# Pooled attention and a gated convolution FFN on one core: six late gates by Sigmoid, two attention tiles with eight exponentials, additions in other pieces, a new order

## The chip, the cores and the metric

One core of one Trainium2 chip. The metric is the device time of one execution in microseconds (us), as the median of several runs. The engines are called as the profile calls them: PE (matrix products; PEld is its loading of weights), DVE (vector), ACT (scalar functions), POOL (general, here mostly the issuer of loads) and SP (issuer of DMAs).

## The reference

Keys and values are averaged over 8 neighbours (576 positions to 72), attention runs over the 72, and its output x goes through a feed-forward block with a gate that is a convolution over three neighbouring positions.

```python
k_p = k.reshape(B, H, Sp, pool, D).mean(axis=3)          # B, H, S, D = 8, 8, 576, 64; pool = 8
v_p = v.reshape(B, H, Sp, pool, D).mean(axis=3)
scores = scale * np.matmul(q, k_p.transpose(0, 1, 3, 2))
scores = scores - np.max(scores, axis=-1, keepdims=True)
attn = np.exp(scores)
attn = attn / (np.sum(attn, axis=-1, keepdims=True) + 1e-09)
x = np.matmul(attn, v_p)                                  # then heads side by side: 576 x 512
h = np.maximum(x @ w_in, 0.0)                             # 512 -> 1024
conv_out[:, s] = sum over k of conv_w[k] * h[:, s + k - 1]
gate = 1.0 / (1.0 + np.exp(-conv_out))
out = (h * gate) @ w_out                                  # 1024 -> 512
```

## The kernel before

**Work and tiles.** The eight batches form four groups g of two. The 1152 rows of a group make nine attention tiles t of 128 rows (group 0 has ten, its middle one cut in two). A tile goes through `att_scores` (PE), `att_max` (DVE, largest score of each of the 8 heads, negated), `att_shift` (subtracts it, by DVE into `sd`, or by PE for the ten tiles of group 0), `att_exp` (ACT), the turn of e (`att_turn` on PE with `att_copy`, or `att_send` by a transposing DMA on SP, groups 2 and 3), `att_values` (PE), `att_divide` (DVE) and the turn of x (`att_turn_out` and `att_copy_out`, or `att_out` on SP) into `xT`.

**The FFN of a batch b.** Its 1024 channels are eight blocks fb of 128, in two halves f4 of four. `ffn_in` (PE) multiplies by w_in, in two halves of 288 columns, `ffn_relu` (ACT) writes `hT`. The convolution has two forms. `ffn_conv` (PE) multiplies by diagonal matrices `dw`; a pair of blocks is written crosswise, so half of the result has its 64-row halves exchanged. `ffn_tap`, for (b, f4) = (4,1), (5,0), (5,1), (6,0), (6,1), (7,0), scales the middle tap on ACT and adds the two others on DVE, in `tg`; before them `ffn_wrap` copies 63 columns at both ends (POOL). Then ACT takes tanh of half the sum (`ffn_tanh`, `ffn_tap_tanh`), DVE adds 1 (`ffn_gate`, which also exchanges the halves back, L892 and L894, or L842) and multiplies by `hT` (L902, L843), into `gT`; `hT` holds half of h, since sigmoid(z) = (1 + tanh(z/2))/2. `ffn_out` (PE, 128 rows by 512 columns, eight products) needs all gates of its batches; ACT or DVE copies the result and SP or ACT issues the stores, two of 128 KB for each tile.

**What sets the order.** Every step is an `Op` of a graph, with its steps before it and its buffers. `Graph.ORDER` is a written list of numbers: 2 x step + engine choice (-1 takes a filling product from the spares), `FORMS` gives the form of some PE steps and `PLACES` the buffer of each ring. The steps are issued in that order; each engine then runs its own in order, held by semaphores. PSUM has eight banks, from which scores, turns, products and convolutions all draw.

**Start.** POOL issues the loads of q, k and v, of w_in and w_out; DVE clears buffers; PE pools the keys of batches 0 and 1 by a matrix `pm` (`prep_k`), keys of the others are added up by DVE (`pool_pair`, L406) and turned on PE.

```python
    def order(self):
        for n in self.ORDER:
            o = spares.pop(0) if n < 0 else self.ops[n // 2]
            o.engine = list(o.engines)[0 if n < 0 else n % 2]
...
    def ffn_tap_gate(b, f4):
        nc.vector.tensor_scalar(out=gate, in0=gate, scalar1=1.0, scalar2=None, op0=OP.add)
        nc.vector.tensor_tensor(out=gate, in0=gate, in1=h_of(b)[:, four], op=OP.mult)
```

## Time and profile before

| what | us |
| --- | --- |
| median of 3 runs (lowest, highest) | 218.12 (217.75, 218.72) |
| the profiled execution | 219.54 |
| its span | 217.8 |
| busy: PE, DVE, ACT, POOL | 198.8, 192.0, 161.8, 45.2 |
| granted clock of PE, mean | 0.998 |

A row of a group reads: line, engine, operation, output <- inputs, shapes, count | busy us, mean ns of one | idle time of the engine just before it, and what ended most of it. A row of the windows reads: stretch, length, then busy us and count of PE, PEld, DVE, ACT and POOL, the granted clock, the DMA share and GB/s. A row of the chain: start, length, what. Issuing of DMAs is not counted as busy; in the timeline it stands as SPq or ACTq. Matmul ends are modelled, so busy PE is not PE at its peak.

### The profile page before, as it was taken

What the parts mean: (1) busy time and instruction counts of PE and PEld (TensorE: products, weight loads), DVE (VectorE), ACT (ScalarE), POOL (GpSimd) and SP (SyncE); (2) the same over time, 40 slices, a digit from 0 to 9 for tenths busy, and PEclk for the clock granted to TensorE, in tenths of its full rate; (3) what the DMA queues carried; (4) which work ended last, traced back from release to release, by engine and by line L of the source; (5) the groups of instructions that cost most, each with busy time, mean ns of one, the idle gap of its engine ahead of it and who ended that gap; (6) DMA issues with size and microseconds to landing.
All of it is one profiled execution on the core that took longest, in us unless ns stands there. A gap on an engine that the chain in (4) does not pass through costs nothing.

```text
span 217.8 us, 6553 instructions
## 1 busy us (share of the span) xinstructions
PE 198.8 (91%) x2704; PEld 137.7 (63%) x2723; DVE 192.0 (88%) x334; ACT 161.8 (74%) x274; POOL 45.2 (21%) x81
## 2 busy tenths in 40 slices
PE   0597999998999999999999999999999999999990
PEld 0465778776587788667686775666566657545550
DVE  6859988999999899999999999899999999999310
ACT  2136677599989889678759877799889989987330
POOL 7951331033203120000000003103115113520000
PEclk9999999999999999999999999999999999999999
DMA  5999999999999998968865544674573555074864
GB/s 68 172 195 207 208 206 209 205 208 206 209 207 196 203 198 125 133 146 128 175 141 109 83 102 87 117 159 89 125 156 71 122 123 127 0 167 94 222 170 123
DMA packets 48834, 32.62 MB, mean 150 GB/s; under 512 B 28300, under 2 KB 44324, under 8 KB 48804
## 3 DMA queue, kind: packets, MB, share of 16 engines
q0 software_dynamic: 16288, 16.26, 45.8%
q1 hardware_dynamic: 31556, 14.50, 33.1%
q10 hardware_dynamic: 960, 1.44, 2.7%
q8 instruction: 21, 0.34, 0.6%
q14 instruction: 9, 0.07, 0.1%
HBM read 32.52 MB, written 9.44 MB: 193 GB/s over the span
## 4 chain that ended last, share of the span: by engine, by line
PE 50%; DVE 28%; ACT 9%; issue 7%; DMA 4%; POOL 1%; DVEq 0%; ACTq 0%; POOLq 0%
PE psum L910 21%; PE psum L694 17%; DVE negm L575 5%; DVE x L664 5%; DVE sd L587 4%; DMA kk<-in_k_dram 4%; ACT qT L501 3%; PE psum L649 3%; DVE gT L894 2%; PE psum L856 2%; DVE gT L902 2%; DVE v L453 2%; DVE r L662 2%; PE psum L624 2%; DVE kk L406 1%
## 5 line engine op out<-in xcount | busy, mean ns | idle before, releaser
L694 PE MATMUL psum<-xT,w_in_sb 128*128 128x288 bf16 x512 | 71.1, 286 | 0.1
L910 PE MATMUL psum<-w_out_sb,gT 128*128 128x512 bf16 (+1 forms) x277 | 65.0, 373 | 1.3 <-issue 0.5
L694 PEld LDWEIGHTS <-w_in_sb 128*128 128x128 bf16 x512 | 47.9, 98 | 14.2 <-issue 0.2
L703 ACT ACTIVATE hT<-psum 128x576 bf16<-128x576 f32 x64 | 40.7, 649 | 11.6 <-PE psum L694 11.1
L910 PEld LDWEIGHTS <-gT 128*128 128x128 bf16 x296 | 27.7, 98 | 27.7 <-issue 0.7
L831 DVE SCALAR_TENSOR_TENSOR tg<-hT,convw,tg 128x576 f32<-128x576 bf16 x48 | 37.7, 816 | 0.8
L575 DVE TENSOR_REDUCE negm<-psum 128x8 f32<-128x576 f32 (+2 forms) x37 | 27.5, 750 | 3.0 <-PE psum L562 1.7
L778 POOL COPY hT<-hT 128x126 bf16<-128x126 bf16 x16 | 9.4, 589 | 94.2 <-ACT hT L703 78.6
L664 DVE TENSOR_TENSOR x<-psum,r 128x512 bf16<-128x512 f32 (+1 forms) x37 | 25.6, 691 | 1.3
L587 DVE TENSOR_TENSOR sd<-psum,negm 128x576 f32<-128x576 f32 x27 | 20.1, 752 | 1.1 <-ACT gT L836 0.5
L856 PE MATMUL psum<-hT,dw 64*64 64x288 bf16 (+2 forms) x608 | 20.0, 261 | 0.5 <-DVE sd L587 0.3
L649 PE MATMUL psum<-vm,eT 128*128 128x65 bf16 (+5 forms) x240 | 19.0, 222 | 0.7 <-DVE vm L457 0.3
L613 ACT ACTIVATE e<-sd 128x576 bf16<-128x576 f32 x27 | 18.3, 689 | 1.1 <-DVE sd L587 1.1
L856 PEld LDWEIGHTS <-dw 64*64 64x64 bf16 x608 | 15.3, 107 | 5.8 <-issue 4.6
L829 ACT ACTIVATE tg<-hT,convw 128x576 f32<-128x576 bf16 x24 | 18.3, 774 | 0.1
L649 PEld LDWEIGHTS <-eT 128*128 128x128 bf16 (+1 forms) x240 | 15.0, 100 | 4.3 <-issue 1.8
L836 ACT ACTIVATE gT<-tg 128x576 bf16<-128x576 f32 x24 | 16.1, 681 | 1.6 <-DVE tg L831 0.9
L921 ACT COPY osb<-psum 128x512 f32<-128x512 f32 x25 | 14.6, 585 | 2.7 <-PE psum L910 2.3
L881 ACT ACTIVATE gT<-psum 128x576 bf16<-128x576 f32 x20 | 12.9, 647 | 3.8 <-PE psum L856 3.8
L881 ACT ACTIVATE tg<-psum 128x576 bf16<-128x576 f32 x20 | 13.0, 648 | 2.5 <-PE psum L856 1.8
L902 DVE TENSOR_TENSOR gT<-gT,hT 128x2304 bf16<-128x2304 bf16 x10 | 13.4, 1352 | 0.1
L453 DVE TENSOR_TENSOR v<-v 128x1280 bf16<-128x1280 bf16 (+2 forms) x24 | 12.9, 539 | 0.2
(83 smaller groups left out, 231.2 us busy)
## 6 DMA issues: line engine op xcount, KB each, us to landing
out_dram<-osb SPq DMA_DIRECT2D x54, 128.0 KB, 2.4
v<-in_v_dram POOLq DMA_DIRECT2D x8, 512.0 KB, 15.6
qp<-in_q_dram POOLq DMA_DIRECT2D x7, 576.0 KB, 13.9
kk<-in_k_dram POOLq DMA_DIRECT2D x3, 1152.0 KB, 13.5
out_dram<-qp ACTq DMA_DIRECT2D x10, 128.0 KB, 2.4
w_in_sb<-in_moe_w_in_dram POOLq DMA_DIRECT2D x2, 512.0 KB, 16.6
w_out_sb<-in_moe_w_out_dram POOLq DMA_DIRECT2D x1, 1024.0 KB, 22.1
out_dram<-qp SPq DMA_DIRECT2D x6, 128.0 KB, 2.4
```

Source lines behind the costliest of these rows:

```text
L575: nc.vector.tensor_reduce(out=a["m"][0:rows], in_=a["s"][0:rows, :, 0:2 * KW].rearrange("p a (h s) -> p a h s", s=Sp), axis=AX.X, op=OP.ma ...
L587: nc.vector.tensor_tensor(out=a["d"][0:rows], in0=a["s"][0:rows, :, 0:2 * KW].rearrange("p a (h s) -> p a h s", s=Sp), in1=a["m"][0:rows]. ...
L613: nc.scalar.activation(out=dst, in_=src, func=ACT.Exp, scale=1.0 / (POOL * 8.0),)
L649: nc.tensor.matmul(out=a["o"][lo:hi, h // 4, (h % 4) * (D + 1):(h % 4 + x1 - x0) * (D + 1)], lhsT=a["eT"][:, j, lo:hi], rhs=buf("vm", b)[: ...
L664: nc.vector.tensor_tensor(out=a["x"][0:rows].rearrange("p (a h d) -> p a h d", a=2, d=D), in0=ov[:, :, :, 0:D], in1=r[0:rows].unsqueeze(3) ...
L694: nc.tensor.matmul(out=banks(ps)[:, j, 0:SC], lhsT=w_in_block(dc, fb), rhs=buf("xT", g)[:, dc, i * S + j * SC:i * S + (j + 1) * SC], start ...
L703: nc.scalar.activation(out=h_of(b)[:, fb].rearrange("p (a s) -> p a s", a=2), in_=banks(ps)[:, :, 0:SC], func=ACT.Relu, scale=0.5,)
L829: nc.scalar.activation(out=acc, in_=h, func=ACT.Identity, scale=w)
L831: nc.vector.scalar_tensor_tensor(out=acc, in0=h, scalar=w, in1=acc, op0=OP.mult, op1=OP.add)
L856: nc.tensor.matmul(out=banks(pss[r ^ c])[c * D:(c + 1) * D, j, lo:hi], lhsT=dw[r * D:(r + 1) * D, tap * n_fb + fb, :], rhs=hT[r * D:(r + 1 ...
L881: nc.scalar.activation(out=t.rearrange("p (a s) -> p a s", a=2), in_=banks(ps)[:, :, 0:SC], func=ACT.Tanh, scale=0.5,)
L910: nc.tensor.matmul(out=bank(ps)[0:rows, columns], lhsT=buf("gT", g)[:, fb, t * P:t * P + rows], rhs=w_out_sb[:, fb, columns], start=(fb == 0),
```

## The change

1. **Six gates by Sigmoid.** The gates of both halves of batches 5, 6 and 7 are made by `ACT.Sigmoid`; `hT` then holds h itself (scale 1.0 in the ReLU), and the addition of 1 falls away. For (7,1), by `ffn_conv`, the exchange of halves stays, as a plain copy. The Sigmoid needs another function table than Exp and Tanh, so ACT loads a table a second time, and all exponentials come ahead of the first Sigmoid.
2. **Two tiles with eight exponentials.** For (g, t) = (3,1) and (3,8) the maximum is not subtracted ahead; ACT takes eight exponentials of 72 columns out of PSUM, each with the head's negated maximum as its bias. Tiles (0,5) and (0,9) go from subtraction by PE to DVE. The scale 1/64 moves from the exponential into the pooled keys.
3. **Additions in other pieces.** The three parts of `ffn_gate` are steps of their own, each on DVE or ACT (there `Identity` with a column of ones as bias). ACT has four of those before batch 4 and one of (7,1).
4. **Other engines and forms.** Six ReLUs run on DVE; five of twelve wraps on ACT; (4,0) and (7,1) are convolved without wraps, with 32 products for a pair of blocks in place of 24; tiles (1,0) and (1,3) turn x by DMA, (2,3) turns e on PE; five stores of the middle part go from SP to ACT; there are 11 filling products in place of 3, all within the start.
5. **ORDER, FORMS and PLACES are written anew**, so steps of all kinds stand at other places.

Counted over the whole program, on DVE: additions `gT<-gT` of 128x2304 from 6 to 1, of 128x1152 from 10 to 8, `gT<-tg` of 64x1152 from 20 to 15 and one copy of that shape. ACT issues 12 DMAs of stores before and 21 after, POOL makes 32 copies for wraps before and 14 after, and SP issues nine DMAs of stores fewer.

The start, on ACT, from its first instruction to the first exponential. Before:

```order
L1018 ACT_TABLE_LOAD
L1018 CAST gT_120<-ident 128x128
L398 CAST kT_80<-psum 64x2x72 x4
L501 COPY qT_77<-psum 128x2x320
L613 ACTIVATE e_96<-psum 128x576
```

With the change:

```order
L1025 ACT_TABLE_LOAD
L1025 CAST gT_120<-ident 128x128
L523 COPY qT_78<-psum 128x2x256
L418 CAST kT_81<-psum 64x2x72 x2
L523 COPY qT_78<-psum 128x2x320
L647 ACTIVATE e_97<-psum 128x576
```

Two of the four casts of the pooled keys (kT) of batch 0 have moved to DVE, and ACT has one more copy of its queries.

The middle part, on ACT, in the FFN of batches 1 and 3 beside the attention of groups 1 and 2. Before:

```order
L613 ACTIVATE e_99<-sd_126 128x576
L881 ACTIVATE gT_119<-psum 128x576
L881 ACTIVATE tg_116<-psum 128x576
L703 ACTIVATE hT_115<-psum 128x576
L613 ACTIVATE e_101<-sd_128 128x576
L703 ACTIVATE hT_115<-psum 128x576 x2
L881 ACTIVATE tg_117<-psum 128x576
L881 ACTIVATE gT_120<-psum 128x576
L921 COPY osb_124<-psum 128x512
```

With the change:

```order
L744 ACTIVATE hT_116<-psum 128x576
L647 ACTIVATE e_97<-sd_127 128x576
L817 ACTIVATE gT_121<-tg_117,ones 64x2x576
L744 ACTIVATE hT_116<-psum 128x576 x2
L946 DMA out_dram<-osb_122 64x512 x2
L883 ACTIVATE gT_120<-psum 128x576
L647 ACTIVATE e_99<-sd_128 128x576
L883 ACTIVATE tg_117<-psum 128x576
L934 COPY osb_125<-psum 128x512
```

An addition with ones and the two DMAs of a store now stand between ReLUs, tanhs and exponentials.

The end, on DVE, from the last multiplication of batch 6 to that of batch 7 (hT_114 is batch 7's before, hT_115 with the change). Before:

```order
L842 TENSOR_SCALAR gT_120<-gT_120 128x4x576
L843 TENSOR_TENSOR gT_120<-gT_120,hT_115 128x4x576
L831 SCALAR_TENSOR_TENSOR tg_117<-hT_114,convw,tg_117 128x576
L831 SCALAR_TENSOR_TENSOR tg_116<-hT_114,convw,tg_116 128x576 x2
L892 TENSOR_SCALAR gT_120<-gT_120 128x2x576
L894 TENSOR_SCALAR gT_120<-tg_118 64x2x576 x2
L842 TENSOR_SCALAR gT_120<-gT_120 128x4x576
L843 TENSOR_TENSOR gT_120<-gT_120,hT_114 128x4x576
L902 TENSOR_TENSOR gT_120<-gT_120,hT_114 128x4x576
```

With the change:

```order
L915 TENSOR_TENSOR gT_120<-gT_120,hT_116 128x4x576 x2
L845 SCALAR_TENSOR_TENSOR tg_117<-hT_115,convw,tg_117 128x576 x2
L845 SCALAR_TENSOR_TENSOR tg_119<-hT_115,convw,tg_119 128x576 x2
L934 COPY qp_73<-psum 128x512
L845 SCALAR_TENSOR_TENSOR tg_117<-hT_115,convw,tg_117 128x576
L845 SCALAR_TENSOR_TENSOR tg_118<-hT_115,convw,tg_118 128x576
L845 SCALAR_TENSOR_TENSOR tg_117<-hT_115,convw,tg_117 128x576
L845 SCALAR_TENSOR_TENSOR tg_118<-hT_115,convw,tg_118 128x576
L934 COPY osb_123<-psum 128x512
L819 COPY gT_120<-tg_119 64x2x576
L915 TENSOR_TENSOR gT_120<-gT_120,hT_115 128x4x576 x2
```

The additions ahead of the multiplications are gone but for one copy of half rows; both multiplications of batch 6 stand ahead of all taps of batch 7, and all its eight taps and two copies of outputs behind them.

The diff, cut to its core (the tables of numbers left out):

```diff
+        "shift": {
+            (0, 0): 1, (0, 1): 1, (0, 2): 1, (0, 3): 1, (0, 4): 1, (0, 6): 1, (0, 7): 1, (0, 8): 1, (3, 1): 2, (3, 8): 2,
+        },
...
+        "sigma": {
+            (5, 0): 1, (5, 1): 1, (6, 0): 1, (6, 1): 1, (7, 0): 1, (7, 1): 1,
+        },
...
     ORDER = (
-        6, 28, 14, 2, 24, 4, 26, 10, 34, 16, 36, 20, 22, 12, 104, 108, 106, 8, 38, 32, 18, 30, 40, 92, 56, 42, 58, -1, 44, 97,
...
+        6, 18, 14, 24, 2, 28, 4, 10, 16, 36, 20, 34, 8, 40, -1, 12, -1, 108, 26, 22, 111, -1, 42, 32, -1, -1, -1, 30, 46, -1,
...
-        nc.vector.memset(pm[0:TB, :, 0:Sp], 1.0)
+        nc.vector.memset(pm()[0:TB, :, 0:Sp], SCALE)
...
     def att_exp(g, t):
         a, rows = att[g, t], rows_of(g, t)
         e = a["e"] = buf("e", g, t)
+        if graph.chosen("shift", g, t) == 2:
+            for x in range(2):
+                for h in range(4):
+                    at = h // 2 * 2 * KW + x * KW + h % 2 * Sp if a["by_rows"] else (4 * x + h) * Sp
+                    nc.scalar.activation(
+                        out=e[0:rows, at:at + Sp],
+                        in_=a["s"][0:rows, x, h * Sp:(h + 1) * Sp],
+                        func=ACT.Exp,
+                        bias=a["m"][0:rows, x, h:h + 1],
+                        scale=1.0,
+                    )
+            return
...
-            scale=1.0 / (POOL * 8.0),
+            scale=1.0,
...
+    def ffn_relu(b, fb, ps, o):
+        out = h_of(b)[:, fb].rearrange("p (a s) -> p a s", a=2)
+        scale = 1.0 if graph.chosen("sigma", b, fb // 4) else 0.5
+        if o.engine == "DVE":
+            nc.vector.tensor_scalar(
+                out=out, in0=banks(ps)[:, :, 0:SC], scalar1=scale, scalar2=0.0, op0=OP.mult, op1=OP.max
+            )
+            return
+        nc.scalar.activation(out=out, in_=banks(ps)[:, :, 0:SC], func=ACT.Relu, scale=scale)
...
+    def ffn_wrap(b, lo, hi, o):
+        t, copy = buf("hT", b)[:, lo:hi], nc.scalar.copy if o.engine == "ACT" else nc.gpsimd.tensor_copy
...
+    def gate_func(b, fb):
+        return ACT.Sigmoid if graph.chosen("sigma", b, fb // 4) else ACT.Tanh
...
+    def raise_gate(engine, b, fb, out, in_, start=0):
+        sigma = graph.chosen("sigma", b, fb // 4)
+        if engine is nc.scalar:
+            rows = slice(start, start + in_.shape[0])
+            nc.scalar.activation(out=out, in_=in_, func=ACT.Identity, bias=0.0 if sigma else ones[rows], scale=1.0)
+        elif sigma:
+            engine.tensor_copy(out=out, in_=in_)
+        else:
+            engine.tensor_scalar(out=out, in0=in_, scalar1=1.0, scalar2=None, op0=OP.add)
...
+    for o in sigmas:
+        for e in exps:
+            graph.follow(e, o)
```

854 lines of the change are left out of this document (405 added, 449 removed), and 100 rows, old and new, of tables (ORDER, PLACES).

## The prediction

> **What bounds the kernel now.** I read the page's head first, then the windows by stage, then the chain, then the startup and the end in the timeline. The head gives the span and each engine's busy time:
>
> ```profile
> span 217.8 us, 6553 instructions
> PE 198.8 (91%) x2704; PEld 137.7 (63%) x2723; DVE 192.0 (88%) x334; ACT 161.8 (74%) x274; POOL 45.2 (21%) x81
> ```
>
> Two engines are near full, so the average says little. By stage (columns: stretch, its length, busy time of PE, PEld, DVE, ACT, POOL, then clock and DMA):
>
> ```profile
> 0.00:13.00 13.00, 5.28 (x59) 3.83 (x60) 8.99 (x31) 2.67 (x6) 11.18 (x23) 1.00 0.91 129
> 13.00:30.00 17.00, 14.78 (x319) 11.19 (x318) 14.34 (x28) 10.75 (x18) 5.82 (x12) 1.00 1.23 207
> 30.00:44.00 14.00, 14.00 (x244) 10.96 (x242) 12.61 (x28) 9.56 (x17) 1.42 (x3) 1.00 1.23 207
> 44.00:58.00 14.00, 12.53 (x281) 9.04 (x281) 13.38 (x22) 13.67 (x24) 5.13 (x7) 1.00 1.24 207
> 58.00:86.00 28.00, 27.27 (x474) 22.07 (x474) 27.09 (x50) 24.79 (x43) 4.41 (x6) 1.00 1.18 194
> 86.00:139.00 53.00, 51.85 (x783) 36.63 (x790) 51.42 (x90) 40.73 (x69) 2.67 (x8) 1.00 0.68 120
> 139.00:203.00 64.00, 63.47 (x510) 39.09 (x518) 62.39 (x88) 56.88 (x96) 14.57 (x24) 1.00 0.52 116
> 203.00:213.00 10.00, 9.59 (x53) 4.91 (x51) 1.62 (x3) 2.71 (x5) 0.00 (x0) 1.00 0.74 189
> ```
>
> The reader is to see four things. Up to 30 us nobody is full: startup latency. From 44 to 58 ACT is (13.67 of 14). From 58 to 139 DVE and PE stand together at 97 to 98%. From 139 on PE has 63.47 of 64 and is the bound. The chain agrees: DVE pieces until 138, then PE alone to the end:
>
> ```profile
> 111.17 0.76 DVE negm L575
> 111.95 0.76 DVE sd L587
> ...
> 187.71 1.73 PE psum L910 x8
> ...
> 201.83 10.77 PE psum L910 x57
> 212.69 0.42 DVE qp L921
> ```
>
> So a microsecond counts if it brings forward the start, takes work from DVE (or PE) before 139, or takes PE work after 139. The last is hardly touched: the late products are the same ones.
>
> **The start.** All attention waits for the pooled keys, made at 10.79 when the second key load lands:
>
> ```profile
> 10.79 1.29 PE L373 MATMUL psum<-gT,kk 128*64 128x144 bf16 x18 [0.75 <-DMA kk<-in_k_dram]
> 12.01 0.93 PE L366 MATMUL psum<-gT 128*128 128x448 bf16 x2
> 12.12 0.56 ACT L398 CAST kT<-psum 64x144 bf16<-64x144 f32 x2 [1.98 <-PE psum L373]
> 12.73 1.17 PE L562 MATMUL psum<-kT,qT 128*128 128x144 bf16 x8
> 13.46 1.42 DVE L575 TENSOR_REDUCE negm<-psum 128x8 bf16<-128x576 f32 x2 [1.69 <-PE psum L562]
> ```
>
> The change issues the loads in the same order up to that landing, so 10.79 stays. After it, the two casts run side by side on ACT and DVE: 0.56 becomes 0.28. The two fill matmuls between keys and scores are gone to earlier places, where PE waits anyway, and one tile's scores (half of 1.17), no longer two, stand ahead of the rest. The first maximum comes 0.28 earlier by the cast and up to 0.2 by the shorter run of scores: **-0.45**. The ends are 0 (something else late) and -0.7.
>
> **DVE.** Prices per instruction, rows of the groups with shapes apart (mean ns):
>
> ```profile
> L842 DVE TENSOR_SCALAR gT<-gT 128x2304 bf16<-128x2304 bf16 x6 | 4.7, 783 | 0.0
> L892 DVE TENSOR_SCALAR gT<-gT 128x1152 bf16<-128x1152 bf16 x10 | 4.5, 452 | 0.1
> L894 DVE TENSOR_SCALAR gT<-tg 64x1152 bf16<-64x1152 bf16 x20 | 9.1, 455 | 0.3
> L664 DVE TENSOR_TENSOR x<-psum,r 128x512 bf16<-128x512 f32 x35 | 24.2, 691 | 1.2
> L587 DVE TENSOR_TENSOR sd<-psum,negm 128x576 f32<-128x576 f32 x27 | 20.1, 752 | 1.1 <-ACT gT L836 0.5
> L703 ACT ACTIVATE hT<-psum 128x576 bf16<-128x576 f32 x64 | 40.7, 649 | 11.6 <-PE psum L694 11.1
> ```
>
> Additions that go: five of 783 (3.92), two of 452 (0.90), five of 455 (2.28), of which one comes back as a plain copy (at most 0.46). What comes: six ReLUs out of PSUM, which DVE has not done before; between 691 (512 columns) and 752 (576 columns, two operands) I take 0.75, together 4.5. The subtractions of the maximum stay 27: tiles (3,1) and (3,8) lose theirs, (0,5) and (0,9) get one. Copies out of PSUM that change hands amount to one of the 691 kind more. Sum: -3.92 - 0.90 - 2.28 + 0.46 + 4.5 + 0.7 = -1.4 of 192.0.
>
> Where it lies decides. The Sigmoid part (the five of 783) and four of the ReLUs are after 139, under PE's cover: worth nothing there. Before 139, three additions of 455 and one of 452 move to ACT (-1.82), two subtractions go (-1.50), two ReLUs come (+1.50) and small copies (+0.4): -1.4. Against it stand the two subtractions (+1.50) that now fall before 40 us; DVE has 2.66 free between 13 and 30, in pieces, so I let half be hidden. Net **-0.6**, from 0 (all of it exposed) to -1.4.
>
> **PE.** The turns of e (L624) and x (L681), and the two forms of the convolution (L856):
>
> ```profile
> 41.12 0.87 PE psum L856 x32
> ...
> 61.11 0.28 PE psum L624 x5
> ...
> 77.61 0.62 PE psum L681 x8
> ...
> 194.24 0.86 PE psum L856 x24
> ```
>
> Two tiles' turns of x go to the DMA (-0.62), one tile's turn of e comes (+0.28); two blocks' convolutions go from 24 pieces to 32, 0.86 against 0.87. With PE at 51.85 of 53 this counts nearly whole: **-0.3** (0 to -0.6). The eight further fills run before 10.79 in idle time.
>
> **ACT and the queues.** Here the change pays:
>
> ```profile
> L398 ACT CAST kT<-psum 64x144 bf16<-64x144 f32 x4 | 1.1, 272 | 6.3 <-DVE ident L354 4.3 <-PE psum L373 2.0
> L425 ACT CAST kT<-psum 64x288 bf16<-64x288 f32 x6 | 2.4, 392 | 0.4 <-DVE kT L425 0.3
> L501 ACT COPY qT<-psum 128x1152 bf16<-128x1152 bf16 x7 | 7.7, 1142 | 1.2 <-PE psum L487 0.7 <-PE psum L483 0.5
> L1018 ACT ACT_TABLE_LOAD x1 | 1.3, 1283 | 0.8 <-PEq L1359 0.8
> L829 ACT ACTIVATE tg<-hT,convw 128x576 f32<-128x576 bf16 x24 | 18.3, 774 | 0.1
> L836 ACT ACTIVATE gT<-tg 128x576 bf16<-128x576 f32 x24 | 16.1, 681 | 1.6 <-DVE tg L831 0.9 <-PE psum L910 0.4
> 200.42 1.20 ACTq L933 DMA_DIRECT2D out_dram<-qp  x2
> ```
>
> Between 86 and 139 ACT gets two additions of 1152 columns (as the row of 1142: 1.1 each, 2.2), five stores that SP issued before (1.20 each by the last row: 6.0), and the eight exponentials twice. From 144 columns at 272 to 288 at 392 a column costs 0.83 ns, so 72 columns are 0.21 and eight are 1.7, against one of 0.69: +2.0. One copy of e more (0.7), two ReLUs and three copies of x fewer (-1.3, -1.9): together +7.7, so 48.4 of 53. A row also shows what a per-partition operand costs: 774 with the weight against 681 without, 0.09. The Trainium skill, page "ScalarE: Activation LUTs", section "What ACT_TABLE_LOAD costs", says the same for a bias taken from a [128,1] operand, about 93 ns, and overlaps that much between neighbours; its formula makes the eight 2.0 and my +2.0 a +2.6, an estimate from that page.
>
> After 139 ACT gets the second table load (1.28), ten small wraps that POOL did (0.27 or less each, 2.6) and one addition (1.1), and loses four ReLUs (2.6) and two copies (1.2): +1.2 on 56.88 of 64, covered. Queued behind the table load are taps and ReLUs of batches 5 and 6; DVE has taps of other blocks meanwhile. The same section of the Trainium skill puts a drain of about 1.38 beside each load, which no row here shows; with it the stage would hold 59.5 of 64, and if load and drain stood bare on the path the time would be the forecast's plus 2.7, 219.5 (0.03, held within A's chance below).
>
> SP loses five stores (6.0) and one send of e and gets two sends of x, so it only gains room. POOL is idle most of the time.
>
> **The end.** The last multiplication ends at 203.61:
>
> ```profile
> 202.26 1.35 DVE L902 TENSOR_TENSOR gT<-gT,hT 128x2304 bf16<-128x2304 bf16 x1
> ```
>
> Five tiles of output follow it, 1.73 each (row above): 8.65 before 212.6, so PE reached them at 203.95. The slack is 0.34. In the new order DVE has, from the multiplications of batch 6 on, eight taps (0.82), two copies (0.68), one copy of half rows (0.46) and two multiplications (1.35): 11.1; PE has eleven half tiles (0.86) and two convolutions (0.87) there: 11.2. So the slack stays about as thin.
>
> **Sum.** -0.45 - 0.6 - 0.3 = -1.35. From the profiled 219.54 (span 217.8 and 1.74 around it) that is 218.2; the runs' median 218.12 lies 1.42 below the profiled one, so **216.8**. A measurement can tell about 0.5% (1.1 us) from no change.
>
> **Rivals.**
> A, slower: ACT becomes the bound between 86 and 139.
>
> ```profile
> ACT hT L703 <- PE psum L694: 5.7, 11, 1.3
> ```
>
> This wait of that stretch lies in ACT's order: ReLUs stand at the head while PE works. If it stays, 48.4 + 5.7 = 54.1 passes 53 by 1.1; with ACT's other waits there kept too (53 - 40.73 = 12.3 idle) it passes by 7.7. The stores make it likelier, as a store holds ACT for 1.2 while exponentials stand behind it. It decides from the point where less than 1.1 of the wait is filled. Price 2.6, nearer the lower end; the savings on DVE and PE are then lost: 218.12 - 0.45 + 2.6 = 220.3. Against it: the new order may put the work just into those waits. By the Trainium skill's price of the eight it would be 220.9. Chance 0.19.
> B, no change: what DVE sheds is behind PE's cover and the exposed part balances; only the start is left: 217.7. For it speaks 63.47 of 64 after 139 and the thin slack at the end. Chance 0.21.
> C, more: the order is new throughout and may close waits besides. DVE is idle 2.66 + 1.39 + 0.62 + 0.91 + 1.58 = 7.2 between 13 and 139; a third of it gives another -2.4: 214.4. Nothing in the rows says that it must. Chance 0.20.
>
> **How the numbers follow.** Forecast 0.40, its own range 215.4 (all three terms at their far ends, -2.7) to 218.1 (all at 0). The range goes to 214.0, under C's centre, and to 219.8, where somewhat over half of A is left out: 214.0 to 219.8. Faster by over 0.5% (under 217.0): 0.33 of the forecast's 0.40 and C's 0.20, 0.53; within: 0.07 and B, 0.28; slower: A, 0.19.
>
> **What would show it.** The start: the first maximum at 13.0 in place of 13.46. DVE: busy about 190.5, at 97% or more from 58 on, the handover to PE near 138. ACT: 86 to 139 with about 48 busy and PE still over 97%; if PE and DVE fall below 95% there while ACT is over 50, A holds. The end: PE without a gap in the last 11 us; a gap before the last five tiles means that the gates of batch 7 came late. The forecast falls if the table load or the ACT stores show up as waits of DVE.

## The result and the profile after

The changed kernel takes 219.31 us (median of 22 runs, 217.82 to 220.58) against 218.09 us (22 runs, 217.56 to 219.57): 1.0053 times the time before, with a 95% interval of 1.0037 to 1.0069. It is slower by 1.2 us. The forecast was 216.8, faster by 1.3; the measured time lies inside the range of 214.0 to 219.8, but on the other side of no change. Of all runs in this document, three slow ones of one kernel (g6_no_fills) are left out of its median and ratio; the others count in full.

The head of the page of the changed kernel:

```profile
span 217.9 us, 6632 instructions
PE 199.4 (92%) x2740; PEld 137.2 (63%) x2740; DVE 190.8 (88%) x331; ACT 168.1 (77%) x295; POOL 35.5 (16%) x64
```

VectorE's busy time came out as forecast (190.8 us, forecast 190.5). The time went elsewhere. The windows of the changed kernel, with the stretch from 86 to 139 parted at 96:

```profile
0.00:13.00 13.00, 7.17 (x80) 4.47 (x82) 8.42 (x32) 2.71 (x5) 11.60 (x23) 1.00 0.94 134
13.00:30.00 17.00, 14.33 (x313) 11.14 (x307) 15.16 (x32) 12.58 (x21) 5.74 (x13) 1.00 1.23 207
30.00:44.00 14.00, 14.00 (x274) 11.27 (x271) 13.27 (x26) 10.10 (x18) 1.30 (x2) 1.00 1.23 207
44.00:58.00 14.00, 11.52 (x252) 8.04 (x252) 13.71 (x24) 13.21 (x23) 5.32 (x7) 1.00 1.24 207
58.00:86.00 28.00, 27.45 (x465) 22.18 (x463) 27.38 (x49) 24.60 (x43) 4.37 (x6) 1.00 1.18 193
86.00:96.00 10.00, 8.69 (x117) 6.32 (x114) 8.29 (x14) 7.36 (x13) 0.00 (x0) 1.00 1.07 163
96.00:139.00 43.00, 42.38 (x659) 29.33 (x656) 40.80 (x73) 36.14 (x71) 2.56 (x4) 1.00 0.68 117
139.00:203.00 64.00, 64.00 (x551) 39.50 (x551) 61.67 (x87) 58.13 (x103) 4.62 (x10) 1.00 0.53 113
```

Two rows stand out. Between 44 and 58 TensorE has 11.52 of 14, where the row of the kernel before in the prediction has 12.53; "The sum" below comes back to it. Between 86 and 96 TensorE has 8.69 of 10 and VectorE 8.29. The kernel before, run again (below), has 9.73 and 9.84:

```profile
86.00:96.00 10.00, 9.73 (x141) 6.83 (x141) 9.84 (x16) 6.46 (x13) 0.00 (x0) 1.00 0.60 129
```

TensorE, VectorE and ScalarE are idle at once there, so something outside them may be late. The timeline there, SP first (SPq and ACTq are the issuing of DMAs; the brackets give the idle time before and its releaser):

```profile
84.59 3.66 SPq L517 DMA_TRANSPOSE qT<-qp  x1
88.30 1.77 SPq L946 DMA_DIRECT2D out_dram<-osb  x2
90.19 1.50 SPq L667 DMA_TRANSPOSE eT<-e  x1
```

```profile
88.59 0.56 ACTq L946 DMA_DIRECT2D out_dram<-osb  x1
88.83 0.63 ACT L744 ACTIVATE hT<-psum 128x576 bf16<-128x576 f32 x1
91.47 0.48 ACTq L946 DMA_DIRECT2D out_dram<-osb  x1
92.05 0.65 ACT L883 ACTIVATE gT<-psum 128x576 bf16<-128x576 f32 x1 [2.59 <-DVE negm L597]
92.75 2.39 PE L728 MATMUL psum<-xT,w_in_sb 128*128 128x288 bf16 x16 [1.20 <-ACT gT L883]
93.44 0.76 DVE L609 TENSOR_TENSOR sd<-psum,negm 128x576 f32<-128x576 f32 x1 [1.17 <-ACT e L647]
```

ScalarE stands still for 2.59 us before 92.05, and the releaser printed there, a maximum of VectorE, ended only shortly before; it is not what ScalarE's queue was waiting for. Between the two halves of one store of ScalarE, issued at 88.59 and at 91.47, lies the hold. The chain of waits in that stretch names it:

```profile
84.59 6.86 DMA qT<-qp
91.44 0.02 issue
91.47 0.48 ACTq L946
```

The store's second half starts 0.02 us after a transfer landed whose data it doesn't touch: the transposing DMA of batch 6's queries, which SP issued. The program shows the link. In it the DMAs of SP and of ScalarE count up eight semaphores in turn when they land, and ScalarE's two halves each wait for one of them:

```
L946 DMA out_dram<-osb_122 64x512 [waits DMAHW0_49]
L946 DMA out_dram<-osb_122 64x512 [waits DMAHW1_49]
```

DMAHW1 is the one that the query DMA counts up when it lands, and the program lets the store's second half go only after that. In the kernel before, the same query DMA starts about nine microseconds later on SP (93.31 in the second execution of it, below), and ScalarE issues no store in this stretch.

The first 14 us answer for the start. TensorE in the changed kernel:

```profile
7.01 2.05 PE L386 MATMUL psum<-gT 128*128 128x448 bf16 x5
...
9.41 2.21 PE L393 MATMUL psum<-gT,kk 128*64 128x144 bf16 x36
```

Five filling products take 2.05 us at 7.01, and the pooled keys (L393, both halves in one row) begin behind them at 9.41 without any wait for a load. So they were not held by their load, but by the fills.

How long these products then take differs from execution to execution. Eleven kernels of this document share this start with seven fills (the changed kernel and the ten variants of it, from e2 to h3 in the table, that leave all fills in). Their keys take 1.29 to 2.32 us, and their first maximum of VectorE lies between 11.56 and 12.77, here at 12.66. The shortest, in e3_adds_dve:

```profile
9.24 1.29 PE L393 MATMUL psum<-gT,kk 128*64 128x144 bf16 x36
```

So a start is read below from all executions that share it, not from one.

### The profile page after: what moved, and what is told of

Read it like the earlier page. It is cut to its first block, busy times and chain, and to the rows that moved or that the text cites. A ratio compares the mean times of both kernels' runs of the same rounds, so it can differ in the third digit from the quotient of the medians.

```text
span 217.9 us, 6632 instructions
## 1 busy us (share of the span) xinstructions
PE 199.4 (92%) x2740; PEld 137.2 (63%) x2740; DVE 190.8 (88%) x331; ACT 168.1 (77%) x295; POOL 35.5 (16%) x64
## 3 DMA queue, kind: packets, MB, share of 16 engines
q10 hardware_dynamic: 1680, 2.69, 5.1%
## 4 chain that ended last, share of the span: by engine, by line
PE 64%; DVE 19%; ACT 6%; issue 5%; DMA 3%; ACTq 0%; DVEq 0%
PE psum L923 27%; PE psum L728 18%; PE psum L868 4%; PE psum L683 4%; DMA qT<-qp 3%; DVE x L698 3%; DVE sd L609 2%; DVE gT L915 2%; DVE kk L425 2%; ACT e L647 2%; DVE gT L821 2%; DVE negm L597 2%; PE psum L584 2%; PE psum L505 2%; PE psum L386 1%
## 5 line engine op out<-in xcount | busy, mean ns | idle before, releaser
L923 PE MATMUL psum<-w_out_sb,gT 128*128 128x512 bf16 (+1 forms) x296 | 66.7, 373 | 0.7 <-DVE gT L915 0.7
L744 ACT ACTIVATE hT<-psum 128x576 bf16<-128x576 f32 x58 | 36.9, 647 | 8.9 <-PE psum L728 7.2
L597 DVE TENSOR_REDUCE negm<-psum 128x8 f32<-128x576 f32 (+3 forms) x37 | 27.3, 750 | 2.3 <-PE psum L571 1.2
L609 DVE TENSOR_TENSOR sd<-psum,negm 128x576 f32<-128x576 f32 (+1 forms) x27 | 20.2, 754 | 1.9 <-ACT e L647 1.2
L915 DVE TENSOR_TENSOR gT<-gT,hT 128x2304 bf16<-128x2304 bf16 x16 | 21.4, 1353 | 0.4 <-ACT gT L817 0.3
L791 POOL COPY hT<-hT 128x126 bf16<-128x126 bf16 x7 | 4.0, 572 | 99.8 <-ACT hT L744 99.8
L647 ACT ACTIVATE e<-sd 128x576 bf16<-128x576 f32 (+1 forms) x27 | 18.3, 686 | 1.4 <-DVE sd L609 1.3
L868 PE MATMUL psum<-hT,dw 64*64 64x288 bf16 (+2 forms) x640 | 19.1, 256 | 0.2 <-DVE x L698 0.2
L934 ACT COPY osb<-psum 128x512 f32<-128x512 f32 x24 | 14.0, 587 | 2.9 <-PE psum L923 2.7
```

What stands on the lines that cost most here:

```text
L597: nc.vector.tensor_reduce(out=a["m"][0:rows], in_=a["s"][0:rows, :, 0:2 * KW].rearrange("p a (h s) -> p a h s", s=Sp), axis=AX.X, op=OP.ma ...
L609: nc.vector.tensor_tensor(out=a["d"][0:rows], in0=a["s"][0:rows, :, 0:2 * KW].rearrange("p a (h s) -> p a h s", s=Sp), in1=a["m"][0:rows]. ...
L647: nc.scalar.activation(out=dst, in_=src, func=ACT.Exp, scale=1.0,)
L744: nc.scalar.activation(out=out, in_=banks(ps)[:, :, 0:SC], func=ACT.Relu, scale=scale)
L868: nc.tensor.matmul(out=banks(pss[r ^ c])[c * D:(c + 1) * D, j, lo:hi], lhsT=dw[r * D:(r + 1) * D, tap * n_fb + fb, :], rhs=hT[r * D:(r + 1 ...
L923: nc.tensor.matmul(out=bank(ps)[0:rows, columns], lhsT=buf("gT", g)[:, fb, t * P:t * P + rows], rhs=w_out_sb[:, fb, columns], start=(fb == 0),
```

## The experiments

The ratio is to the kernel before, on the same chip.

| run | what it is | median us | ratio (95%) |
| --- | --- | --- | --- |
| e1_before_again | before, once more | 218.14 | one run |
| e2_stores_sp | after, middle stores on SP | 220.38 | 1.0104 (1.0066 to 1.0141) |
| e3_adds_dve | after, middle additions on DVE | 219.69 | 1.0067 (1.0041 to 1.0093) |
| e4_tanh | after, Tanh and additions again | 222.99 | 1.0213 (1.0181 to 1.0245) |
| f1_store_first | after, ACT's store earlier | 218.43 | 1.0031 (1.0006 to 1.0056) |
| f2_one_dma | after, a store in one DMA | 322.76 | 1.4807 (1.4779 to 1.4835) |
| f3_relu_act | after, all ReLUs on ACT | 219.62 | 1.0077 (1.0047 to 1.0107) |
| f4_one_exp | after, one exponential a tile | 220.39 | 1.0092 (1.0065 to 1.0120) |
| g1_before_fills | before with 8 early fills | 219.13 | 1.0039 (1.0025 to 1.0054) |
| g3_sigma_before | before with the Sigmoid part | 218.30 | 0.9999 (0.9987 to 1.0012) |
| g5_qsend_late | after, query DMA late | 217.96 | 0.9989 (0.9970 to 1.0007) |
| g6_no_fills | after, no early fills | 219.43 | 1.0042 (1.0012 to 1.0073) |
| h1_both_q_late | g5, second query DMA late too | 220.66 | 1.0130 (1.0094 to 1.0166) |
| h3_q_late_stores_sp | g5, middle stores on SP | 220.31 | 1.0098 (1.0074 to 1.0121) |
| h4_q_late_two_fills | g5 with two of seven fills | **216.66** | **0.9936 (0.9922 to 0.9951)** |
| h6_before_q_early | before, query DMA earlier | 218.28 | 1.0006 (0.9994 to 1.0018) |
| i1_two_fills | after with two of seven fills | 218.53 | 1.0020 (0.9997 to 1.0042) |
| i2_h4_adds_relu_back | h4, additions and ReLUs back | 218.33 | 1.0019 (1.0002 to 1.0037) |

### Before, run again

No edit. The profile that the prediction rests on is of an execution of 219.54 us, long for this kernel, so it was run and profiled once more.

> The kernel before, unchanged, profiled a second time: its first profiled execution (219.54) lay 1.4 above the median of its runs, so its rows may show a late start that most of its runs don't have. Theory 1 (the changed kernel starts earlier, and loses more than that behind it): in this second execution the first maximum lies again near 13.46 or at most 0.4 earlier, and from 86 to 96 DVE and PE stay at 97% or more. Theory 2 (the earlier start of the changed kernel is only the luck of one execution): the first maximum lies near 12.7 here too, and the span is about 216.4, all of the difference to the first profile lying ahead of the first maximum.

It took 218.14, with a span of 216.4. TensorE's start:

```profile
8.41 1.29 PE L373 MATMUL psum<-gT,kk 128*64 128x144 bf16 x18 [1.33 <-DVE gT L314]
...
10.12 1.29 PE L373 MATMUL psum<-gT,kk 128*64 128x144 bf16 x18
```

The second half of the keys runs at 10.12, not at 10.79, and waits for no load; the first maximum is at 12.78 instead of 13.46. Two variants below with the same start (g3 and h6) have the second half at 9.97. The wait for the load in the prediction's row belonged to that one execution. The first maxima of the four executions with the old start are 13.46, 12.78, 12.64 and 12.23: by the medians, the changed kernel's start with seven fills (12.21) is 0.5 ahead of the old one (12.71).

That lead is not kept. A later step that both kernels have, the turn of pooled keys on TensorE (L412, with the change L431), starts at 43.58 to 45.56 with the old start (median 44.25) and at 43.77 to 45.03 with the new one (median 44.43).

### Whose hold: the store, the query DMA, or ScalarE's load

**e2_stores_sp** gives the five stores of the middle stage back to SP.

```diff
+        if g < 3:
+            queue = nc.sync
```

> The changed kernel with the five output stores between 88 and 141 issued by SP again and not by ACT; nothing else moves. Theory 1 (the second half of the first such store is held for 2.3 us while SP's transposing DMAs are under way, ACT stands behind it from 89.46 to 92.05, DVE then waits 1.17 and PE 1.20): the hole goes, PE has 8.9 of 9 busy between 87 and 96 instead of 7.70, and the time falls by 1.0 to 1.6, to about 218.0. Theory 2 (the stores don't matter, ACT's additions and other work do): within 0.3 of the changed kernel. Theory 3 (SP has no room, the stores then hold back the turns of e and x on SP): slower than the changed kernel by 0.3 or more.

The hold at 91 went, although the query DMA is as early as in the changed kernel (TensorE 9.79 of 10 between 86 and 96). Yet the time rose to 220.38: SP has no room for the stores. TensorE there:

```profile
119.65 0.32 PE L571 MATMUL psum<-kT,qT 64*64 64x72 bf16 x15 [1.29 <-ACT osb L934]
```

The copy into `osb` waits for a store that SP issued at 115.79 and that landed at 118.9, and scores wait for the copy. So the five stores are cheaper on ScalarE than on SP.

**f1_store_first** puts ScalarE's store ahead of a ReLU, an exponential, an addition and two more ReLUs, in ScalarE's order; SP's own order stays.

```diff
 L883 ACTIVATE tg_117<-psum 128x576
+L946 DMA out_dram<-osb_122 64x512 x2
 L744 ACTIVATE hT_116<-psum 128x576
 ...
 L744 ACTIVATE hT_116<-psum 128x576 x2
-L946 DMA out_dram<-osb_122 64x512 x2
```

> The changed kernel with its first ACT store (two DMAs at 88.59 and 91.47) written ahead of the transposing DMA of q in the order and nothing else moved. In the trace of the changed kernel the second of the two DMAs waits for the very semaphore that the transposing DMA of q counts up when it lands (91.45), and takes it over: eight such counters serve the DMAs of SP and ACT in turn. Theory 1 (this wait for a counter costs the time: ACT 2.6, then DVE 1.17 and PE 1.48 in three instances of the order): the hole in PE at 91 goes, PE is busy 9.7 of 10 or more from 86 to 96, and the time falls by 0.8 to 1.4 against the changed kernel, to about 218.2. Theory 2 (SP has too much to issue between 84 and 120; what one hole loses another takes, as when the five stores went back to SP and the hole came at 118): the hole goes, but the time falls by less than 0.4, and PE stands more between 100 and 120.

218.43, ratio 1.0031: better than after's 1.0053, though the intervals overlap. The store's second half then goes at 85.42, and ScalarE's wait before its next tanh shrinks from 2.59 to 1.03. So the wait on ScalarE belongs to the pair of store and query DMA, not to the exponentials. But TensorE gains only 0.24 in the window, and has a new wait:

```profile
86.00:96.00 10.00, 8.93 (x119) 6.60 (x118) 8.55 (x15) 8.33 (x15) 0.00 (x0) 1.00 1.15 158
...
95.02 0.89 PE L683 MATMUL psum<-vm,eT 128*128 128x130 bf16 x12 [0.76 <-DMA eT<-e]
```

It waits for a send of e. SP issued that send at 90.59, behind the query DMA and a store, and it landed after 4.4 us. So the early query DMA costs in two ways: by the counter that it shares with the store, and by what stands behind it on SP. With the first taken away, the second shows.

**g5_qsend_late** moves the query DMA instead, on SP, behind one store, two sends of e and two of x:

```diff
-L517 DMA_TRANSPOSE qT_78<-qp_76 128x18x128
 L946 DMA out_dram<-osb_123 64x512 x2
 L667 DMA_TRANSPOSE eT_105<-e_97 128x5x128
 ...
 L667 DMA_TRANSPOSE eT_104<-e_98 128x5x128
+L517 DMA_TRANSPOSE qT_78<-qp_76 128x18x128
```

> The changed kernel with the transposing DMA of q for batch 6 moved back on SP behind one output store, two turns of e and two of x, so about where the kernel before has it (94.7 there, 84.6 in the changed kernel); all else as in the changed kernel, its stores on ACT too. Theory 1 (SP is held 3.7 us by this DMA while the loads still fill the DMA engines, and everything behind it on SP and the counter it holds comes late: PE stands 1.48 at 91): the DMA takes 2 to 3 us to issue at its new place, PE is busy 9.7 of 10 from 86 to 96, no hole of over 0.6 there or up to 120, and the time falls by 1.0 to 1.6, to 217.8 to 218.3. Theory 2 (holes in this stretch only move, as with the store written first: 0.6 won of 1.5): 0.3 to 0.8 faster. Theory 3 (not this DMA): within 0.3.

217.96, ratio 0.9989: 0.64% (1.4 us) under the changed kernel, by one moved DMA. SP and ScalarE of g5 at the same place:

```profile
92.25 2.80 SPq L517 DMA_TRANSPOSE qT<-qp  x1
```

```profile
88.95 0.79 ACTq L946 DMA_DIRECT2D out_dram<-osb  x1
90.25 0.65 ACT L883 ACTIVATE gT<-psum 128x576 bf16<-128x576 f32 x1 [1.03 <-PE psum L868]
```

The store's second half is issued at 88.95, not at 91.47, and TensorE is busy for all of 86 to 96:

```profile
86.00:96.00 10.00, 10.00 (x162) 7.25 (x163) 9.53 (x17) 8.92 (x15) 0.00 (x0) 1.00 0.70 140
```

This shows what the early place of the query DMA costs. How the 1.4 us divide between the shared counter and the sends behind the DMA on SP is not shown: f1, which takes away only the first, lies between the two kernels, and its interval touches both.

**h6_before_q_early** asks whether the early query DMA harms by itself. In the kernel before, it goes ahead of two sends of e:

```diff
+L495 DMA_TRANSPOSE qT_79<-qp_72 128x18x128
 L633 DMA_TRANSPOSE eT_103<-e_97 128x5x128
 L633 DMA_TRANSPOSE eT_102<-e_96 128x5x128
-L495 DMA_TRANSPOSE qT_79<-qp_72 128x18x128
```

> The kernel before, with the transposing DMA of batch 6's queries alone put earlier on SP, ahead of two sends of e instead of behind them (SP starts it at about 88.5 us instead of 93.3), while the key and value loads still fill the DMA engines. If the early DMA by itself costs time (it holds SP for 3.7 us as in the changed kernel, the sends of e behind it go late, and ScalarE's store that shares a counter with it waits): slower than before by 0.3 to 1.3 us, with a hole of over 0.5 us on TensorE between 88 and 96. If it costs only together with the new order around it: within 0.3 us of before, and no such hole.

218.28, ratio 1.0006: no difference, and TensorE has 10.00 of 10 between 86 and 96.

```profile
90.24 1.94 SPq L495 DMA_TRANSPOSE qT<-qp  x1
```

It started only at 90.24, 5.7 later than in the changed kernel, so it is a weak test of an early DMA. What it shows is that at this later time the DMA passes two sends of e at no cost, in a kernel where ScalarE has no store that shares a counter with it.

**h3_q_late_stores_sp** joins g5's move and e2's edit.

> g5 with the five stores of the middle stage issued by SP instead of ScalarE. If ScalarE's stores cost something beyond the one wait at 91 us: faster than g5 by 0.3 us or more. If SP has no room for them (it issues DMAs for 31 to 33 of 36 us there): slower than g5 by 0.5 us or more, with holes of TensorE before output projections that wait for a store's landing, as in e2_stores_sp at 118 us.

220.31, 1.1% over g5: on SP the stores lose time with the query DMA late too, and more than the 0.5% by which e2 lies over the changed kernel. What the stores still cost on ScalarE is not tested.

**h1_both_q_late** also moves the second query DMA, behind two more sends of e:

```diff
-L517 DMA_TRANSPOSE qT_80<-qp_75 128x18x128
 L667 DMA_TRANSPOSE eT_105<-e_98 128x5x128
 L667 DMA_TRANSPOSE eT_104<-e_99 128x5x128
+L517 DMA_TRANSPOSE qT_80<-qp_75 128x18x128
```

> The changed kernel with both transposing DMAs of the queries later on SP: the first as in g5_qsend_late, the second behind two further sends of e. If the second one also holds SP where TensorE waits: TensorE's hole of 0.52 us at 110.5 goes, and the time is 0.2 to 0.6 us under that of g5 (217.96). If TensorE's other waits take its place: within 0.3 us of g5.

A miss: 220.66, 2.7 us over g5, outside both expectations. The hole at 110.5 went, and a greater one came. SP and TensorE of h1:

```profile
107.55 3.35 SPq L517 DMA_TRANSPOSE qT<-qp  x1
...
115.44 1.22 SPq L946 DMA_DIRECT2D out_dram<-osb  x2
```

```profile
119.31 0.32 PE L571 MATMUL psum<-kT,qT 64*64 64x72 bf16 x15 [1.77 <-ACT osb L934]
```

3.35 us of issuing now stand ahead of a send of e, two of x and a store at 115.44; the next copy into `osb` waits for that store, and TensorE waits 1.77 for the copy. It is the hole of e2, reached in another way: 3.35 us of SP's time between 100 and 120, given away at a wrong place, cost more than the hole that they closed.

### The start

**g6_no_fills** takes all seven early fills out of the changed kernel (seven entries less in the order).

> The changed kernel without its seven empty matmuls ahead of the pooled keys; nothing else. Theory 1 (the start is kept): the pooled keys take 2.5 in place of 1.29 to 2.21, the first maximum comes 0.3 to 1.2 later than with them, and the time is 0.3 to 1.2 longer than the changed kernel's. Theory 2 (the new order loses the start again between 13 and 30): the first maximum is later, the time within 0.3 of the changed kernel.

219.43, the same as after within the intervals. The keys start at 7.83. Both expectations had the first maximum later than with the fills; at 11.67 it is not. But TensorE is then slow:

```profile
7.83 2.69 PE L393 MATMUL psum<-gT,kk 128*64 128x144 bf16 x36 [0.50 <-DVE gT L331]
...
11.57 1.28 PE L505 MATMUL psum<-ident,qp 128*64 128x128 bf16 x20
```

The 20 turns of queries take 1.28 here and 0.75 in all eleven executions with seven fills ahead. So none may be too few, though the time doesn't part it from seven.

**g1_before_fills** puts eight fills into the kernel before, ahead of the keys, and the clearing of what they read to the front of VectorE's order.

> The kernel before with eight of the empty matmuls of the changed kernel's start put ahead of its first keys, where PE waits, and the memset that they read first on DVE; nothing else. In the traces, 36 matmuls of the pooled keys take 2.58 in the kernel before and 1.29 to 2.21 in runs of the changed kernel, which has such matmuls ahead of them. Theory 1 (a start made earlier is kept to the end, PE being the bound from 28 on): the two groups of keys take 0.65 to 0.9 each in place of 1.29, the first maximum comes at 11.8 to 12.3 in place of 12.78, and the time falls by 0.4 to 0.9, below the kernel before. Theory 2 (what the start gains is lost again by 30, as in the changed kernel, where the loads or the latency of the first tiles set the pace): the first maximum comes earlier, the time stays within 0.3.

219.13, slower by 0.39%, which neither expectation had. Six of them take 2.42 us at 7.41, and the keys move from 8.41 to 9.76; the first maximum, at 13.01, lies within the spread of the old start. In the old order too, such fills do not run in idle time.

**h4_q_late_two_fills** is g5 with the first two fills left and the five at 7.01 gone (five entries -1 less in the order).

> g5 with only two of the seven early filling matmul groups left ahead of the keys. If what is won at the start is lost again before 30 us, where TensorE becomes the bound: first maximum at about 11.6 us instead of 12.4, and the time within 0.3 us of g5 (217.96). If the start counts once the hold at 91 us is gone: 0.3 to 0.8 us under g5.

216.66, ratio 0.9936: the one version clearly faster than both kernels, by 0.64% than before and by 1.2% than after, and 0.53% (1.2 us) faster than g5, more than either expectation. Its start:

```profile
7.91 2.51 PE L393 MATMUL psum<-gT,kk 128*64 128x144 bf16 x36
...
11.46 0.91 PE L505 MATMUL psum<-ident,qp 128*64 128x128 bf16 x20
```

The first maximum stands at 11.56, and at 11.46 and 11.52 in the two other executions with two fills (i2 and i1). The turn of pooled keys starts at 43.24 to 43.81 in these three, 1.0 ahead of seven fills by the medians. So what two fills win over seven is still there at 44 us.

**i1_two_fills** is the changed kernel with the same five fills gone and the query DMA left early.

> The changed kernel with only two of its seven early filling matmul groups, and the transposing DMA of batch 6's queries where the change put it. If the late start (five fills ahead of the keys) and the hold at 91 us are two separate losses that add: the first maximum at about 11.7 us, TensorE's hole at 90 stays, and the time is 1.1 to 1.5 us under the changed kernel's 219.31, so 217.8 to 218.2. If the hold at 91 us takes back what is won before it, as in g6_no_fills (219.83): within 0.4 us of 219.31.

218.53, ratio 1.0020: between the two expectations. Of the 1.05 us by which this execution of i1 is ahead of that of the changed kernel at 44 us (the turn of pooled keys, L431, at 43.81 against 44.86) only 0.6 is left behind the hold. The end of the hold is not set by the kernel's progress but by the query DMA, and that waits on SP until its queries have been loaded. The chains of i1 and (above) of the changed kernel agree on its start within 0.12 us:

```profile
84.47 6.37 DMA qT<-qp
...
90.86 0.48 ACTq L946
```

The store goes at 90.86 here and at 91.47 there. The four kernels make a square, as ratios to before:

| | query DMA early | query DMA late |
| --- | --- | --- |
| seven fills | 1.0053 (after) | 0.9989 (g5) |
| two fills | 1.0020 (i1) | 0.9936 (h4) |

The early query DMA is worth 0.64% and 0.84% (1.4 and 1.8 us), the five fills 0.33% and 0.53% (0.7 and 1.2 us). Each looks worth more where the other is mended, but that difference of 0.2% is within the intervals. Together they are 1.17%, 2.5 us.

### What the edits in the arithmetic are worth

**e3_adds_dve** gives the middle additions (batches below 4) back to VectorE.

```diff
     def raise_gate(engine, b, fb, out, in_, start=0):
+        if b < 4:
+            engine = nc.vector
```

> The changed kernel with its four early additions of one to the gates (three of 64x1152, one of 128x1152; 1.25 each on ACT) done by DVE again in the same places (0.46 each). Theory 1 (the hole at the store is the loss, the additions are covered): within 0.4 of the changed kernel, rather slower, since DVE gets 1.8 more before 139 and ACT has room. Theory 2 (ACT's added work between 83 and 110 delays the exponentials that DVE and PE wait for): faster by 0.6 or more.

219.69 (1.0067 against after's 1.0053): the intervals overlap; no verdict.

**f3_relu_act** gives VectorE's six ReLUs back to ScalarE.

```diff
-        if o.engine == "DVE":
+        if False:
```

> The changed kernel with its six ReLUs on DVE (0.75 each) done by ACT again in the same places (0.65 each): two lie ahead of 139, four behind. If DVE is the engine that sets the end ahead of 139, as the prediction took it to be, 1.5 less on DVE makes the time 0.5 to 1.5 shorter; if ACT's waits set it there (theory 1 and 2 of the stores), ACT gets 1.3 more in the disputed stretch and the time stays within 0.4 or grows.

219.62 (1.0077): again higher than after, and again with intervals that overlap.

**f4_one_exp** replaces the eight exponentials of tiles (3,1) and (3,8) by a subtraction of VectorE in place and one exponential.

```diff
-            for x in range(2):
-                for h in range(4):
...
-            return
+            s = a["s"][0:rows, :, 0:2 * KW].rearrange("p x (h k) -> p x h k", h=4)
+            nc.vector.tensor_tensor(
+                out=s, in0=s, in1=a["m"][0:rows].unsqueeze(3).to_broadcast([rows, 2, 4, Sp]), op=OP.add
+            )
```

> The changed kernel with the two tiles of eight exponentials done as before by one subtraction on DVE (0.75, here written back into PSUM) and one exponential on ACT (0.69 in place of eight of 0.36, 1.8 net of their overlap). ACT gets about 2.2 less between 86 and 139, DVE 1.5 more. If ACT is what runs late in that stretch (rival A of the prediction): faster by 0.5 to 1.5. If DVE is: slower by 0.5 to 1.5. If neither, because the waits lie at SP's DMAs: within 0.4.

220.39 (1.0092), from four runs: the two tiles' eight exponentials are no loss. Their price in the changed kernel:

```profile
L634 ACT ACTIVATE e<-psum,negm 128x72 bf16<-128x72 f32 x16 | 3.6, 364 | 0.0
```

One lasts 0.364, but neighbours overlap: the 16 together keep ScalarE busy for 3.6, so a tile's eight take 1.8.

**i2_h4_adds_relu_back** joins e3's and f3's edits, on top of h4, where no hold hides them.

> h4_q_late_two_fills (216.66 us) with two savings of the change undone: the additions of the middle batches' gates on VectorE again instead of ScalarE, and all ReLUs on ScalarE. If VectorE's savings are on the path once start and hold are mended: slower than h4 by 0.5 to 1.0 us. If TensorE alone sets the pace from 28 us on: within 0.3 us of h4, which leaves the whole gain of h4 over before to the start.

218.33, ratio 1.0019: 1.7 us over h4, more than the higher expectation. TensorE's remaining work after 203 us tells the two apart, in h4 (first) and i2 (second):

```profile
203.00:213.00 10.00, 6.94 (x41) 3.68 (x38) 0.42 (x1) 2.72 (x5) 0.00 (x0) 1.00 0.75 198
```

```profile
203.00:213.00 10.00, 8.76 (x48) 4.52 (x48) 1.01 (x2) 2.71 (x5) 0.00 (x0) 1.00 0.76 190
```

i2 is ahead of h4 by 0.24 at 43 us (L431 at 43.24 against 43.48) and has 1.82 more left at 203. So in this order the additions and the ReLUs are on the path. Which of the two carries how much stays open.

**g3_sigma_before** makes five of the six late gates of the kernel before by Sigmoid, without their addition, in the old order.

```diff
+    def sigma(b, f4):
+        return (b, f4) in ((5, 0), (6, 0), (6, 1), (7, 0), (7, 1))
...
+        if not sigma(b, f4):
             nc.vector.tensor_scalar(out=gate, in0=gate, scalar1=1.0, scalar2=None, op0=OP.add)
```

> The kernel before, in its own order, with Sigmoid in five of the six late blocks of gates (all those whose gates stand behind the last exponential), without their additions on DVE: a second table load of 1.28 on ACT, and 0.78 less on DVE four times and 0.45 less once, all behind 139. The prediction's step (worth nothing there, PE covers it): within 0.4 of the kernel before, PE from 139 to 203 still over 63 of 64. Rival (the table load or the wait of gates shows on the path): slower by 0.5 to 2.7. Other rival (DVE near the end was the limit after all): faster by 0.5 or more.

218.30, ratio 0.9999. VectorE falls from 61.63 (e1) to 57.80 in the window and TensorE is as busy as before:

```profile
139.00:203.00 64.00, 63.42 (x493) 38.06 (x491) 57.80 (x80) 57.23 (x97) 14.14 (x24) 1.00 0.52 115
```

3.8 us less on VectorE there are worth nothing in the old order, and the second table load that comes with it costs nothing.

**e4_tanh** takes the Sigmoid part out of the changed kernel and adds the 1 on VectorE.

```diff
-        scale = 1.0 if graph.chosen("sigma", b, fb // 4) else 0.5
+        scale = 0.5
...
-        return ACT.Sigmoid if graph.chosen("sigma", b, fb // 4) else ACT.Tanh
+        return ACT.Tanh
...
+            nc.vector.tensor_scalar(out=part, in0=part, scalar1=1.0, scalar2=None, op0=OP.add)
```

> The changed kernel with the six late gates by Tanh and an addition on DVE ahead of each multiplication, so without the second table load; the order is otherwise that of the changed kernel. DVE gets back 5 times 0.78 and once 0.45, 4.4 in all, less the slack of 2.3 that it has from 139 to 203. Theory 1 (the Sigmoid part costs nothing and relieves DVE, which also has four ReLUs there now): slower than the changed kernel by 0.5 to 2.5. Theory 2 (the second table load or the wait of the gates for the last exponential is what the changed kernel loses): within 0.3 or faster.

222.99, slower than after by 1.6%, more than expected. The changed kernel's order puts the last multiplications at VectorE's end with nothing to spare, so additions there fall on the path:

```profile
204.55 0.75 DVE L918 TENSOR_SCALAR gT<-gT 128x2304 bf16<-128x2304 bf16 x1
205.34 1.36 DVE L919 TENSOR_TENSOR gT<-gT,hT 128x2304 bf16<-128x2304 bf16 x1
```

```profile
206.84 2.32 PE L927 MATMUL psum<-w_out_sb,gT 128*128 128x512 bf16 x12 [1.89 <-DVE gT L919]
```

The new order needs the Sigmoid part; the old one gains nothing by it.

### A failed edit

**f2_one_dma** issues a store of two halves as one DMA, to free a counter and an issue.

```diff
+            queue.dma_start(
+                out=out[b].rearrange("(p c) d -> c p d", c=C)[c:c + 2, :, columns],
+                in_=osb[0:2 * TB, columns],
+            )
```

> The changed kernel with both halves of an output store in one DMA instead of two (not where a tile spans two batches), on whichever queue issues it; this halves the number of stores' DMAs and moves which counter each DMA gets. Theory 1 (the wait for a counter at 91): unclear in time, the hole at 91 goes if the store then gets another counter; 0 to 1.4 faster. Theory 2 (SP's and ACT's time to issue is what is short between 84 and 120, 31 of 36 us on SP): faster by 1.5 or more, since each store frees about 0.6 on its queue and PE's holes from 86 to 120 close. If one DMA of 128 rows takes as long to issue as two of 64, no change.

322.76 us. It tells nothing of the hold: sends of e landed after 12.67 us (89.60 to 102.27 in its chain) and stores after 8.37, against 3.4 and 2.4 in the changed kernel's list of DMA issues. Why this form lands so late was not looked into.

## Why the prediction was wrong, point by point

**The sign was wrong by one step that put a cost at nothing; a second such step kept the mended order from a gain.**

1. *"SP loses five stores (6.0) and one send of e and gets two sends of x, so it only gains room."* This step failed. It counted how much SP issues and not what was moved past what. The new order starts the query DMA at 84.59, about nine microseconds ahead of e1's 93.31. It lands at 91.45, a store of ScalarE, new in this stage, waits for the counter that it holds, and the sends of e behind it on SP come late. Measured price of the early place 1.4 us (after against g5), 1.8 with two fills (i1 against h4): more than the whole forecast gain of 1.35.

2. *"The eight further fills run before 10.79 in idle time"*, with *"so 10.79 stays"*. This failed too. The landing at 10.79 was that of one long execution; in the others no load holds the keys. Five of the fills stand in front of the keys and hold them for 1.5 us (7.91 against 9.41), and they cost 0.7 to 1.2 us of time.

**The start, -0.45.** By the medians of all executions the first maximum does come 0.5 earlier (12.21 against 12.71), about as forecast; in the single profile of the changed kernel it is 12.66. That this size came out is luck, since it rested on the landing at 10.79. And the step from an earlier first maximum to a shorter time failed: at 44 us the new order is 0.2 behind the old one (44.43 against 44.25).

**VectorE, -0.6 (0 to -1.4).** The busy time was right (190.8 for 190.5). What it was worth to the old order stays open. Undoing additions and ReLUs in h4 costs 1.7 us (i2), beyond the far end of the range; but what undoing costs in an order written around the pieces is not what they gained, as the Sigmoid part shows: 1.6% when taken out of the new order (e4), nothing when put into the old one (g3). In the changed kernel single pieces show as 0.14%, 0.24% and 0.39% more when undone (e3, f3, f4), each with intervals that overlap.

**ScalarE between 86 and 139.** Forecast 48.4 of 53, measured 43.5 busy. The forecast counted five stores at 1.20, and the profile doesn't count issuing as busy; four of the five fall into the stretch and take 5.1 us, so the two agree at 48.6. An addition took 1.25 instead of 1.1. The eight exponentials took 1.8, for 1.7 in the sum. The Trainium skill, page "ScalarE: Activation LUTs", section "What ACT_TABLE_LOAD costs", by whose formula the eight were 2.0, is a little high here. The drain of 1.38 that it puts beside each table load is not to be seen in this case; the second load stands with 0.02 us on either side of it:

```profile
154.78 1.44 ACT L843 ACTIVATE tg<-hT,convw 128x576 f32<-128x576 bf16 x2
156.24 1.28 ACT L850 ACT_TABLE_LOAD   x1
157.54 0.68 ACT L850 ACTIVATE gT<-tg 128x576 bf16<-128x576 f32 x1
```

**Rival A** named the right place and the right sign, and that the stores on ScalarE would be the trouble. Its mechanism was not the one: ScalarE did not become the bound by its load (43.5 of 53 busy, 48.6 with the stores). One store held it, by a counter. That the time lies inside the stated range is owed to this rival, for whose sake the range went up to 219.8. The check that the prediction set, TensorE and VectorE under 95% with ScalarE over 50, would not have found it: over 86 to 139 TensorE has 51.1 of 53, 96%, and VectorE 93%. A window of 10 us shows it plainly.

**The Sigmoid part, worth nothing after 139:** right for the old order (g3); the new order rests on it (e4). **The handover at the end:** thin, as said; e4 shows that an addition there falls on the path. **TensorE, -0.3:** not tested by itself; open.

**The sum.** With both failed steps mended the change gives 216.66 (h4), beside the forecast 216.8. That is partly chance: in h4 the start is better than forecast (first maximum 11.56), and the new order gives some of it back, since i2 has h4's start and still stands 0.2% over the kernel before. One place where it does so shows in the traces. From 30 to 58 us TensorE is busy for 26.46 to 26.65 in the five executions with the old order, and for 25.42 to 25.53 in those with the new one, h4 and i2 among them. In the new order it waits there for VectorE's additions of keys, for a copy of queries and for a multiplication of gates, here in the changed kernel:

```profile
44.86 0.47 PE L431 MATMUL psum<-pick,kk 128*64 128x64 bf16 x18 [0.83 <-DVE kk L425]
49.41 0.48 PE L509 MATMUL psum<-ident,qp 64*64 64x64 bf16 x36 [0.71 <-ACT qT L523]
52.76 1.90 PE L923 MATMUL psum<-w_out_sb,gT 128*128 128x512 bf16 x8 [0.65 <-DVE gT L915]
```

What closing these waits would be worth was not tested.

## What to carry to other kernels

When an order is written anew, go through each issuing queue and list which DMA passed which, what its transfer competes with at its new time, and whose completion counter it occupies; busy shares and sums of issues show none of this. Idle time ahead of a late load is free for filling work only if the load is late in every execution, so profile a second one before a wait of the first is called fixed. The same holds for a start: here the first maximum of one and the same start moved by 1.2 us between executions. And when two engines issue DMAs, a wait in front of a store can be another engine's transfer, as at 91 us here: the chain named it where the printed releaser didn't.
